# Loading an attention's values as fp32 rows and casting them on the engines, in a fused attention and MoE kernel with a hand-made order of work

## The chip, the cores and the metric

The kernel runs on one core of a Trainium2 chip. A core has five engines that each run their own list of instructions in order: TensorE (PE in the profile; its weight loads are shown as PEld), VectorE (DVE), ScalarE (ACT), GpSimd (POOL) and SyncE (SP). Sixteen DMA engines move data between HBM (the chip's DRAM) and SBUF (the core's memory, 128 partitions); PSUM is the small memory of eight banks into which TensorE writes. The metric is the device time of one execution in microseconds, as a median over runs.

## The reference

Two layers follow each other. First comes attention with a window, for 8 batches, 8 heads, 576 positions and 64 numbers a head:

```
scores = q @ k^T / sqrt(64) - slope[h] * |i - j|       where 0 <= i - j < 128, else -1e9
attn   = softmax(scores)                               per row
x      = attn @ v      -> transposed and reshaped to (8*576 = 4608 tokens, 512)
```

Then comes a feed-forward layer with a gate of its own:

```
h   = x @ w_in                                         (4608, 2048)
g   = h * sigmoid(beta * h)                            beta: one number for each of 2048 columns
out = g @ w_out                                        (4608, 512), float32
```

All inputs and the output are float32. The kernel multiplies in bf16 and accumulates in float32.

## The kernel before

The program is one long list of steps, the string PLAN (lines 18 to 126). A step such as `H:2:4:0` or `gv.s:1:0` names a helper, its engine where there is a choice (`.s` SyncE, `.p` GpSimd, `.v` VectorE, `.a` ScalarE) and its numbers. The loop at the end (line 716) goes through the list and issues each step on its engine. The place of a step in the list therefore sets the order on each engine, and nothing else reorders the work: an engine waits at a step until the data or the buffer that the step needs is there, and everything behind the step on that engine waits with it.

Attention works on one batch after the other. A batch has five blocks of positions, four of 128 and one of 64.

- **Queries and keys.** `gq` and `gk` (`get`, line 306) load a block of all heads as fp32 rows with a SyncE DMA into one of 14 buffers, tile `fst`. `cQ` and `cK` cast it to bf16 (`move`, line 205) on any of three engines. `D` (line 500) is a transposing DMA, also on SyncE, into `qkT`. In batches 0 and 1, which stand at the start, loads of head pairs (`k`, `q`, line 315) and transposes on TensorE (`Rk`, `Rq`) take their place.
- **Values.** In batches 0 to 2, `gv` loads fp32 rows into the same 14 buffers through SyncE, and `cv` casts them into `vs` (line 205). In batches 3 to 7 one step, `pv` (line 342), is a DMA issued by GpSimd that reads fp32 and writes bf16 straight into `vs`. There are two `vs` tiles; batch b writes the one that batch b-2 used, so both `cv` and `pv` wait until batch b-2 has been read.
- **Scores and weights.** `S` (line 522) multiplies, `E` (line 531) takes the exponential on ScalarE, `M` (lines 261 and 275) multiplies by the slopes' factors on VectorE, `V` (lines 574 and 577) multiplies with the values, `n` (lines 585 and 586) divides by the sums on VectorE, and `XD` (line 620) is a transposing DMA on SyncE that writes the tokens into `XT`, a ring of three groups of 512 tokens.

The feed-forward layer works on nine groups of 512 tokens. `H` (line 632) makes one of 16 column blocks of h with four matmuls of 512 columns; `a` (line 640, ScalarE) and `d` (line 645, VectorE) apply the gate; `O` (line 655) takes four matmuls of 512 columns for a quarter of a 128-token block of the output; `oc` (lines 677 and 679) copies it out of PSUM and `st` (line 684) stores it, from three engines. `OL` (line 666) is the last block in two halves. The weights come in eight GpSimd DMAs of 512 KB, `w1` (line 350) and `w2` (line 354), each needed by the first `H` or `O` that reads its part. `pad` (lines 285 to 287) is five memsets on GpSimd. `z` are matmuls on zeros that keep TensorE busy at the start.

So SyncE's queue carries most loads, all transposing DMAs of both kinds and some stores in one order, GpSimd's queue carries the weights, the casting loads of values and some stores, and TensorE's list mixes attention of batch b with the feed-forward layer of earlier tokens.

Of the kernel before, what the change touches and what calls it, by code (L numbers as in the profile page):

```python
# [18 lines left out]
k.s:0:2 const ck.a:0:2 k.s:0:0 k.s:0:1 q.s:0:0 beta:4 k.s:1:0 ck.p:0:0 cq.v:0:0 ones ck.a:0:1 z:2:2  # L19
q.s:0:1 ck.a:1:0 z:2:1 q.s:0:2 q.s:0:3 Rk:0:0:3 Rk:0:1:6 z:1:4 z:1:2 k.s:1:3 gv.s:0:1 k.s:0:3  # L20
cq.v:0:1 Rk:0:2:0 Rk:1:0:1 rk.a:0:0 Rq:0:1:2 cq.v:0:2 rq.a:0:1 Rq:0:2:3 q.s:1:0 q.s:1:1 ck.p:1:3
ck.p:0:3 rq.a:0:2 rk.v:0:1 rk.v:0:2 Rq:0:0:4 B:0:1:6:0 rk.v:1:0 rq.a:0:0 B:0:0:4:0 A:0:2:2:1 EB:0:1
MB:0:1 cv.p:0:1 fr:2 cq.v:1:0 cq.a:0:3 A:0:0:6:1 EB:0:0 EA:0:2 z:2:0 gv.s:0:0 EA:0:0 B:0:2:0:1
cv.p:0:0 Rk:0:3:5 MB:0:0 fr:6 A:0:1:2:1 Rq:0:3:4 Rk:1:3:6 rq.v:0:3 rk.a:0:3 B:0:3:4:1 EA:0:1 EB:0:2
cq.v:1:1 EB:0:3 w1:0 Rq:1:1:7 rk.v:1:3 VA:0:0:3 VA:0:1:0 Rq:1:0:2 VA:0:2:6 A:0:3:4:1 nA:0:0 order
rq.v:1:1 gv.s:0:3 rq.a:1:0 cv.p:0:3 gv.s:0:2 B:1:0:1:0 k.s:1:1 q.s:1:3 cv.p:0:2 w1:1 nA:0:1 nA:0:2
VB:0:2:7 EA:0:3 VB:0:3:5 nB:0:2 ck.a:1:1 VB:0:1:4 VB:0:0:3 Rk:1:1:0 A:1:0:6:1 EB:1:0 nB:0:0 cq.p:1:3
q.s:1:2 nB:0:1 cq.p:1:2 rk.a:1:1 k.s:1:2 EA:1:0 XP:0:2:3 XP:0:0:2 w1:2 VA:0:3:4 gq.s:0:4 xc.a:0:0
nB:0:3 nA:0:3 Rq:1:3:1 XP:0:1:0 xc.v:0:2 A:1:1:5:1 rq.a:1:3 XP:0:3:1 pad ck.p:1:2 EA:1:1 A:1:3:3:1
B:1:1:6:0 xc.a:0:1 xc.a:0:3 h:0:0:5:0:3 EB:1:1 fr:7 fr:5 fr:4 EA:1:3 MB:1:0 H:0:2:1 gv.s:1:2  # L30
h:0:0:5:3:4 h:0:1:7:0:3 H:0:3:2 Rq:1:2:3 h:0:1:7:3:4 Rk:1:2:6 MB:1:1 a:0:2 a:0:3 d:0:2 fr:3 gv.s:1:1
fr:1 rk.v:1:2 a:0:0 H:0:7:1 gv.s:0:4 gk.s:0:4 H:0:6:4 H:0:4:6 gv.s:1:0 d:0:3 d:0:0 fr:0 cQ.a:0:4
fl:0 a:0:7 rq.a:1:2 cv.p:1:2 A:1:2:2:1 a:0:6 d:0:7 a:0:4 H:0:10:5 gv.s:1:3 H:0:5:0 gk.s:1:4 a:0:1
H:0:8:1 d:0:6 EA:1:2 d:0:4 a:0:10 w1:3 a:0:5 ft cK.p:0:4 cv.p:0:4 d:0:1 cv.p:1:0 a:0:8 cv.a:1:1
B:1:2:2:1 d:0:10 EB:1:2 H:0:9:5 VA:1:2:6 gq.s:1:4 d:0:5 d:0:8 gv.s:2:4 gv.s:2:1 gk.s:2:0 VA:1:0:1
TT:0:7 H:0:11:4 cv.p:1:3 a:0:9 VA:1:1:0 a:0:11 nA:1:2 tt.v:0 nA:1:0 d:0:9 B:1:3:6:1 EB:1:3 VB:1:2:5
SCT:0:1 nA:1:1 w2:0 VB:1:0:0 gv.s:1:4 gq.s:2:0 VA:1:3:3 d:0:11 ECT:0 gk.s:2:1 cK.p:2:1 VB:1:1:4
gk.s:2:2 cv.p:1:4 H:0:14:7 nB:1:2 nB:1:1 h:0:15:1:0:2 cQ.a:1:4 gq.s:2:4 gk.s:2:4 a:0:14 cK.a:1:4
VB:1:3:4 w2:1 h:0:15:1:2:4 XP:1:1:2 nA:1:3 MCT:0 PV:0:0:6 nB:1:0 XP:1:2:3 PV:0:1:5 gq.s:2:2 cQ.p:2:2
xc.a:1:1 d:0:14 XP:1:0:0 xc.a:1:0 xc.a:1:2 TT:1:2 nV:0:1 nV:0:0 nB:1:3 a:0:15 H:0:12:7 H:0:13:0  # L40
tt.v:1 w2:2 X:0:4:3 a:0:13 XP:1:3:4 x.v:0:4 d:0:13 xc.a:1:3 SCT:1:5 H:1:7:2 ECT:1 a:1:7 H:1:14:0
d:0:15 a:0:12 fl:2 d:1:7 H:1:9:6 H:1:12:1 a:1:12 d:0:12 gq.s:2:1 gq.s:2:3 d:1:12 H:1:3:4 H:1:5:5
H:1:4:1 a:1:3 a:1:9 H:1:1:3 H:1:10:2 a:1:5 d:1:3 H:1:0:7 a:1:4 a:1:14 d:1:4 w2:3 a:1:1 a:1:10
cK.v:2:2 O:0:0:0:4 d:1:5 d:1:14 d:1:1 cQ.v:2:0 cQ.p:2:1 cv.p:2:4 d:1:10 cK.v:2:0 D:2:0 d:1:9
H:1:15:0 H:1:2:1 gq.s:3:1 D:2:2 a:1:2 a:1:0 H:1:13:5 cv.v:2:1 cQ.a:2:4 O:0:2:0:2 H:1:6:3 O:0:2:1:2
H:1:8:6 O:0:0:1:4 O:0:0:2:4 d:1:0 a:1:6 a:1:13 cK.a:2:4 gk.s:2:3 D:2:1 d:1:2 d:1:13 MCT:1 d:1:6
gv.s:2:0 O:0:2:2:2 O:0:3:0:3 gq.s:3:0 H:1:11:7 a:1:8 a:1:15 a:1:11 d:1:8 cQ.v:2:3 cv.p:2:0 d:1:15
gk.s:4:0 cQ.p:3:1 cK.v:2:3 d:1:11 O:0:0:3:4 O:0:2:3:2 O:0:3:1:3 D:2:4 D:2:3 S:2:0:0:0 S:2:0:1:5
oc.v:0:2 O:1:0:0:2 O:1:0:1:2 gv.s:2:3 E:2:0:1 E:2:0:0 gk.s:3:4 st.s:0:2 O:0:3:2:3 S:2:0:2:6 oc.v:0:0
S:2:0:3:4 PV:1:1:0 gk.s:3:0 E:2:0:3 O:1:0:2:2 E:2:0:2 gq.s:3:2 nV:1:1 fl:4 gv.s:2:2 M:2:0:3 M:2:0:2  # L50
O:0:3:3:3 fl:3 oc.v:0:3 S:2:1:3:4 E:2:1:3 M:2:0:1 fl:1 S:2:1:2:0 S:2:1:0:6 E:2:1:0 O:1:0:3:2
oc.a:1:0 M:2:1:3 E:2:1:2 S:2:1:1:4 M:2:0:0 gq.s:3:4 cv.p:2:2 cQ.v:3:0 M:2:1:0 O:0:1:0:3 E:2:1:1
PV:1:0:6 O:0:1:1:3 gq.s:4:1 gk.s:3:2 gk.s:4:4 gq.s:3:3 V:2:0:0 nV:1:0 cQ.p:3:4 M:2:1:2 O:1:1:0:2
V:2:1:4 n:2:0 O:1:2:0:7 gk.s:3:1 O:1:2:1:7 n:2:1 cQ.p:3:2 M:2:1:1 O:1:1:1:2 X:1:4:6 XD:2:0 XD:2:1
cv.a:2:3 pv:3:1 V:2:2:0 n:2:2 XD:2:2 O:1:2:2:7 O:1:1:2:2 V:2:3:4 O:1:2:3:7 x.a:1:4 cK.v:3:4
O:0:1:2:3 cK.v:3:0 n:2:3 oc.a:1:2 O:0:1:3:3 O:1:1:3:2 cK.v:3:2 cK.v:3:1 gk.s:3:3 st.a:0:0 V:2:4:5
H:2:4:0 H:2:1:7 D:3:0 D:3:2 n:2:4 gq.s:4:2 H:2:10:4 a:2:1 a:2:4 oc.a:0:1 D:3:1 oc.v:1:1 gk.s:4:2
H:2:3:1 H:2:5:6 d:2:4 H:2:2:0 d:2:1 H:2:0:7 D:3:4 a:2:5 H:2:7:3 st.s:1:0 a:2:10 d:2:10 a:2:2 a:2:3
cQ.p:4:1 a:2:0 a:2:7 gq.s:4:0 cK.p:3:3 cQ.v:3:3 d:2:2 d:2:5 d:2:3 H:2:9:4 O:1:3:0:2 a:2:9 cQ.p:4:0
S:3:0:0:5 S:3:0:2:0 O:1:3:1:2 d:2:0 d:2:7 gk.s:5:4 D:3:3 st.a:0:1 O:1:3:2:2 E:3:0:0 E:3:0:2  # L60
S:3:0:1:6 d:2:9 S:3:0:3:3 H:2:6:5 gk.s:4:1 H:2:11:1 O:1:3:3:2 H:2:8:0 E:3:0:1 pv:3:2 E:3:0:3 a:2:6
S:3:1:1:6 a:2:11 a:2:8 XD:2:3 H:2:12:4 E:3:1:1 d:2:6 d:2:11 cK.p:4:2 pv:3:0 cQ.v:4:2 a:2:12 H:2:13:5
d:2:8 M:3:0:1 d:2:12 oc.v:1:3 cK.p:4:0 S:3:1:0:0 E:3:1:0 H:2:14:6 M:3:0:3 M:3:0:2 S:3:1:3:3 a:2:14
S:3:1:2:0 d:2:14 E:3:1:3 O:2:0:0:2 O:2:0:1:2 E:3:1:2 D:4:0 gq.s:4:3 H:2:15:7 M:3:1:3 st.p:0:3
cK.p:4:1 pv:3:4 M:3:0:0 cQ.p:4:3 pv:4:0 st.p:1:2 a:2:15 a:2:13 M:3:1:1 M:3:1:0 d:2:15 O:2:2:0:3
O:2:0:2:2 pv:3:3 V:3:0:0 O:2:1:0:6 n:3:0 cK.v:4:4 d:2:13 M:3:1:2 O:2:1:1:6 V:3:1:0 n:3:1 O:2:1:2:6
V:3:2:4 O:2:1:3:6 n:3:2 gk.s:4:3 D:4:1 D:4:2 gq.s:4:4 gk.s:5:3 cK.v:4:3 cQ.p:4:4 O:2:0:3:2 O:2:2:1:3
st.a:1:1 oc.a:2:1 S:4:0:1:6 pv:4:1 S:4:0:3:4 S:4:0:2:0 E:4:0:1 O:2:2:2:3 E:4:0:3 O:2:3:0:7 E:4:0:2
XD:2:4 XD:3:0 XD:3:2 XD:3:1 oc.v:2:0 D:4:4 D:4:3 O:2:2:3:3 V:3:3:4 V:3:4:0 n:3:3 O:2:3:1:7 oc.v:2:2
O:2:3:2:7 n:3:4 H:3:2:4 H:3:0:2 a:3:2 S:4:0:0:5 d:3:2 a:3:0 gq.s:5:2 gq.s:5:0 M:4:0:1 H:3:7:0  # L70
E:4:0:0 d:3:0 a:3:7 O:2:3:3:7 H:3:1:5 d:3:7 oc.a:2:3 a:3:1 S:4:1:2:2 S:4:1:0:0 M:4:0:2 st.s:2:0
cQ.p:5:2 S:4:1:1:6 gk.s:5:1 E:4:1:0 d:3:1 E:4:1:1 H:3:6:4 H:3:4:5 a:3:6 E:4:1:2 H:3:3:1 XD:3:4
M:4:0:3 M:4:0:0 V:4:0:6 H:3:9:0 a:3:4 d:3:6 n:4:0 V:4:1:3 gq.s:5:1 XD:3:3 H:3:5:2 gk.s:5:2 pv:4:2
st.s:1:3 gq.s:5:3 H:3:12:7 gq.s:7:4 gk.s:5:0 XD:4:0 cK.a:5:1 a:3:3 n:4:1 a:3:9 M:4:1:0 H:3:8:3
XD:4:1 d:3:4 a:3:8 S:4:1:3:5 H:3:15:4 cK.p:5:2 E:4:1:3 d:3:3 pv:4:3 pv:4:4 a:3:12 d:3:9 H:3:14:0
a:3:14 a:3:5 d:3:8 pv:5:1 M:4:1:2 d:3:14 d:3:5 H:3:10:3 H:3:11:1 H:3:13:5 a:3:10 a:3:13 gq.s:5:4
H:4:1:2 H:4:4:6 H:4:2:0 cQ.p:5:3 a:3:11 cK.a:5:0 cQ.a:5:1 M:4:1:3 d:3:12 d:3:13 O:3:1:0:5 H:4:0:7
cQ.v:5:0 d:3:11 a:4:1 cK.p:5:3 cQ.p:5:4 D:5:2 a:3:15 st.s:2:1 a:4:2 gq.s:6:2 a:4:0 d:3:10 D:5:0
# [671 lines left out]
```

## Time and profile before

| | us |
|---|---|
| median of 3 runs (lowest to highest) | 324.43 (323.64 to 325.98) |
| the profiled execution | 323.59 |
| its span | 321.8 |
| TensorE busy | 307.9 (96%) |
| VectorE, ScalarE, GpSimd busy | 198.1, 186.3, 62.9 |
| value loads by GpSimd, 25 instructions | 21.1 |
| casts by GpSimd, 33 into `bst` and 12 into `vs` | 21.0 and 7.9 |

The span runs from the first to the last instruction of the program; the execution has 1.8 us around it. A busy TensorE is not TensorE at its full rate: the profile counts a matmul as busy from its issue to its modelled end, and matmuls overlap. The time to landing of a DMA counts from its issue by the engine, so it holds the wait behind the transfers ahead of it in the queue as well.

### The profile page before, as it was taken

The page shows a single profiled execution, that of the slowest core. Times are in us where ns is not written, and L with a number is a line of the kernel's source. Part 1 is how long each engine was busy: PE and PEld are TensorE (multiplying, and loading weights), DVE is VectorE, ACT ScalarE, POOL GpSimd, SP SyncE. Part 2 cuts the span into 40 slices and gives each one's busy share as a digit, 9 for nine tenths or more (in the row PEclk, how much of TensorE's full clock was granted, in tenths as well). Part 3 has the DMA queues.
Part 4 walks back from the last instruction along what each step waited for, and adds up shares of the span by engine and source line. Part 5 has one row for each costly group of instructions (what it writes and reads, how often), then busy time and mean ns, then how long its engine had stood idle before and what let it go on. Part 6 is the DMA issues. An engine that isn't in the chain of part 4 may idle for free.

```text
span 321.8 us, 5879 instructions
## 1 busy us (share of the span) xinstructions
PE 307.9 (96%) x2218; PEld 152.2 (47%) x2257; DVE 198.1 (62%) x391; ACT 186.3 (58%) x278; POOL 62.9 (20%) x101
## 2 busy tenths in 40 slices
PE   8899999979989999899999999999999999999995
PEld 3464554434544445354455444544544544444543
DVE  4789886843856494588755645752876536865102
ACT  7999786615407854479565664746469324773010
POOL 2372404101301631242050143112000000000000
PEclk9999999998999999999999999999999999999999
DMA  7999999999999999999999899599651134000023
GB/s 243 281 250 199 194 202 187 180 210 223 201 167 233 189 201 172 202 226 179 210 152 230 149 178 138 71 174 182 84 103 35 51 70 152 1 33 2 33 83 147
DMA packets 152684, 50.01 MB, mean 155 GB/s; under 512 B 140288, under 2 KB 148752, under 8 KB 152656
## 3 DMA queue, kind: packets, MB, share of 16 engines
q1 hardware_dynamic: 122512, 37.24, 63.2%
q0 software_dynamic: 28384, 9.51, 27.4%
q10 hardware_dynamic: 1760, 2.89, 2.5%
q8 instruction: 17, 0.28, 0.4%
q14 instruction: 11, 0.09, 0.1%
HBM read 36.71 MB, written 9.44 MB: 143 GB/s over the span
## 4 chain that ended last, share of the span: by engine, by line
PE 74%; DMA 12%; SPq 6%; DVE 2%; POOL 2%; issue 2%; ACT 1%; POOLq 0%; ACTq 0%
PE PS L632 33%; PE PS L655 30%; DMA XT<-xn 6%; PE PS L522 4%; DMA fst<-in_q_dram 3%; DMA fst<-in_k_dram 2%; SPq L500 2%; PE PS L577 2%; SPq L315 2%; PE PS L574 2%; SPq L306 1%; DMA qkT<-bst 1%; PE PS L666 1%; DVE bst L205 1%; PE PS L453 1%
## 5 line engine op out<-in xcount | busy, mean ns | idle before, releaser
L632 PE MATMUL PS<-XT,W 128*128 128x512 bf16 x558 | 132.3, 379 | 3.5 <-DMA XT<-xn 2.3
L640 ACT ACTIVATE sig<-PS,beta_h 128x512 bf16<-128x512 f32 x144 | 94.4, 688 | 68.6 <-PE PS L632 61.9
L655 PE MATMUL PS<-W,gT 128*128 128x512 bf16 x540 | 131.7, 382 | 1.4 <-issue 0.5
L645 DVE SCALAR_TENSOR_TENSOR gT<-sig,PS 128x512 bf16<-128x512 bf16 x144 | 94.0, 683 | 57.1 <-ACT sig L640 56.7
L632 PEld LDWEIGHTS <-W 128*128 128x128 bf16 x576 | 54.2, 98 | 66.9 <-issue 4.2
L655 PEld LDWEIGHTS <-gT 128*128 128x128 bf16 x560 | 52.6, 98 | 61.5 <-issue 3.7
L531 ACT ACTIVATE pt<-PS 128x1024 bf16<-128x1024 f32 x48 | 47.0, 1023 | 22.5 <-PE PS L522 22.1
L205 POOL CAST bst<-fst 128x512 bf16<-128x512 f32 (+1 forms) x33 | 21.0, 644 | 102.4 <-DMA fst<-in_q_dram 36.1
L677 ACT ACTIVATE osb<-PS 128x512 f32<-128x512 f32 (+1 forms) x20 | 11.3, 576 | 33.6 <-PE PS L655 24.0
L342 POOL DMA_DIRECT2D vs<-in_v_dram x25 | 21.1, 847 | 26.4 <-PE PS L577 26.4
L684 POOL DMA_DIRECT2D out_dram<-osb x9 | 5.1, 576 | 88.5 <-DVE osb L679 84.0
L679 DVE TENSOR_SCALAR osb<-PS 128x512 f32<-128x512 f32 x17 | 11.4, 686 | 17.2 <-PE PS L655 17.2
L586 DVE TENSOR_TENSOR xn<-PS,zb 128x512 bf16<-128x512 f32 (+1 forms) x30 | 20.7, 690 | 1.0
L275 DVE TENSOR_TENSOR pt<-pt,fall 128x1024 bf16<-128x1024 bf16 x24 | 16.0, 684 | 4.8 <-ACT pt L531 4.8
L585 DVE RECIPROCAL zb<-PS 128x8 f32<-128x8 f32 (+1 forms) x30 | 6.1, 202 | 19.0 <-PE PS L577 18.4
L205 DVE CAST bst<-fst 128x512 bf16<-128x512 f32 (+1 forms) x28 | 12.6, 455 | 7.1 <-DMA fst<-in_q_dram 2.7
L577 PE MATMUL PS<-vs,pt 128*128 128x65 bf16 x240 | 16.9, 193 | 0.0
L261 DVE TENSOR_TENSOR pt<-pt,falls 128x1024 bf16<-128x1024 bf16 x24 | 16.3, 700 | 0.9 <-ACT pt L531 0.8
L522 PE MATMUL PS<-qkT 64*128 64x256 bf16 (+2 forms) x240 | 14.9, 250 | 2.0 <-DMA qkT<-bst 1.8
L577 PEld LDWEIGHTS <-pt 128*128 128x128 bf16 x240 | 14.6, 97 | 3.5 <-DVE pt L275 0.2
L431 ACT ACTIVATE pt<-PS 128x1024 bf16<-128x1024 f32 (+1 forms) x16 | 14.3, 931 | 0.8 <-PE PS L421 0.6
L522 PEld LDWEIGHTS <-qkT 64*128 64x128 bf16 x240 | 8.7, 94 | 12.6 <-issue 12.1
(73 smaller groups left out, 171.9 us busy)
## 6 DMA issues: line engine op xcount, KB each, us to landing
fst<-in_k_dram SPq DMA_DIRECT2D x32, 256.0 KB, 4.8
fst<-in_q_dram SPq DMA_DIRECT2D x32, 256.0 KB, 5.2
out_dram<-osb SPq DMA_DIRECT2D x16, 256.0 KB, 3.1
fst<-in_v_dram SPq DMA_DIRECT2D x12, 256.0 KB, 6.2
vs<-in_v_dram POOLq DMA_DIRECT2D x20, 128.0 KB, 6.3
out_dram<-osb ACTq DMA_DIRECT2D x10, 256.0 KB, 3.0
out_dram<-osb POOLq DMA_DIRECT2D x9, 256.0 KB, 4.0
W<-in_moe_w_in_dram POOLq DMA_DIRECT2D x4, 512.0 KB, 9.0
```

Of the source, the lines that this page charges most:

```text
L205: (nc.scalar.copy if eng is nc.scalar else eng.tensor_copy)(out=out, in_=in_)
L261: nc.vector.tensor_tensor(out=pt[:], in0=pt[:], in1=falls[:, 2 * p : 2 * p + 2], op=ALU.mult)
L275: nc.vector.tensor_tensor(out=x, in0=x, in1=bass.AP(tensor=t.tensor, offset=t.offset, ap=[list(t.ap[0]), [P, 4], [0, 2], [1, P]]), op=ALU. ...
L342: return nc.gpsimd.dma_start(out=VS[b % 2][0:rows, sb, :, 0:D], in_=v[b, :, P * sb : P * sb + rows, :].rearrange("h p d -> p h d"))
L522: nc.tensor.matmul(o, lhsT=qk[64 * e : 64 * e + 64, 1, p, P * kb : P * kb + P], rhs=qk[64 * e : 64 * e + 64, 0, p, P * kb : P * kb + nq], ...
L531: nc.scalar.activation(out=pt[:], in_=held.pop(("S", b, m, p)), func=ACTF.Exp, scale=qscale)
L577: nc.tensor.matmul(o, lhsT=weights(b, qb, h, 0), rhs=vs[:, qb, h, 0 : D + 1], start=qb == 0, stop=True, skip_group_check=True)
L586: nc.vector.tensor_tensor(out=xn[0:nq].rearrange("p (g h) d -> p g h d", g=2), in0=pv[0:nq, :, :, 0:D], in1=zs[0:nq].broadcast_to([nq, 2, ...
L632: nc.tensor.matmul(hps, lhsT=W1[:, c, bass.ts(j, P)], rhs=XT[:, c, c0 : c0 + TOKG], start=(c == 0), stop=(c == NDM - 1),)
L640: nc.scalar.activation(out=sig[:], in_=hps, func=ACTF.Tanh, scale=beta_h[:, j : j + 1])
L645: nc.vector.scalar_tensor_tensor(out=gts[g][:, j, :], in0=held.pop(("H", g, j))[:], scalar=1.0, in1=hs.pop((g, j)), op0=ALU.add, op1=ALU.mult)
L655: nc.tensor.matmul(ops_, lhsT=gT[:, j, i * P : i * P + P], rhs=W2[:, j, :], start=(j == 0), stop=(j == NFF - 1),)
```

## The change

Only the list is different; no helper is touched. Its counts change as follows.

| steps | before | after |
|---|---|---|
| `pv`, casting loads of values by GpSimd | 25 | 0 |
| `gv.s`, loads of values as fp32 rows by SyncE | 15 | 40 |
| `cv` on GpSimd, VectorE, ScalarE | 12, 1, 2 | 24, 10, 6 |
| `cQ` and `cK` on GpSimd, VectorE, ScalarE | 27, 23, 14 | 31, 16, 17 |
| `st` on SyncE, GpSimd, ScalarE | 16, 9, 10 | 10, 14, 11 |
| `oc` on VectorE, ScalarE | 17, 18 | 20, 15 |

The work of TensorE is the same set of steps in both lists. Since the whole list was made anew, the order of all engines differs from the first step on. The lines of the diff that the prediction speaks of (removed and added ones, each group in its own order):

```
-nB:0:3 nA:0:3 Rq:1:3:1 XP:0:1:0 xc.v:0:2 A:1:1:5:1 rq.a:1:3 XP:0:3:1 pad ck.p:1:2 EA:1:1 A:1:3:3:1
...
-cK.v:2:2 O:0:0:0:4 d:1:5 d:1:14 d:1:1 cQ.v:2:0 cQ.p:2:1 cv.p:2:4 d:1:10 cK.v:2:0 D:2:0 d:1:9
-H:1:15:0 H:1:2:1 gq.s:3:1 D:2:2 a:1:2 a:1:0 H:1:13:5 cv.v:2:1 cQ.a:2:4 O:0:2:0:2 H:1:6:3 O:0:2:1:2
-H:1:8:6 O:0:0:1:4 O:0:0:2:4 d:1:0 a:1:6 a:1:13 cK.a:2:4 gk.s:2:3 D:2:1 d:1:2 d:1:13 MCT:1 d:1:6
...
-V:2:1:4 n:2:0 O:1:2:0:7 gk.s:3:1 O:1:2:1:7 n:2:1 cQ.p:3:2 M:2:1:1 O:1:1:1:2 X:1:4:6 XD:2:0 XD:2:1
-cv.a:2:3 pv:3:1 V:2:2:0 n:2:2 XD:2:2 O:1:2:2:7 O:1:1:2:2 V:2:3:4 O:1:2:3:7 x.a:1:4 cK.v:3:4
...
+rq.v:0:2 ck.p:0:1 cq.p:0:1 pad A:0:2:1:1 B:0:2:4:1 EA:0:2 rk.a:0:0 Rq:0:0:3 Rk:0:1:6 Rq:0:1:7
...
+q.s:1:3 B:0:3:1:1 w1:0 EB:0:3 Rk:1:0:7 gq.s:0:4 A:0:3:3:1 z:2:5 Rq:1:0:6 gq.s:1:4 VB:0:1:2 fr:3
...
+gk.s:2:0 d:1:10 gv.s:1:4 gk.s:2:4 gk.s:3:1 a:1:6 a:1:12 cK.a:2:2 cK.a:2:0 a:1:4 cv.v:1:4 d:1:6
+cQ.v:2:4 H:1:7:4 w2:1 cK.p:2:1 d:1:12 w2:2 w2:3 O:0:0:0:7 D:2:2 H:1:13:3 H:1:8:6 a:1:7 d:1:4 H:1:0:0
+gk.s:2:3 H:1:1:2 D:2:1 a:1:13 a:1:1 H:1:5:1 O:0:0:1:7 a:1:8 cQ.p:2:0 d:1:13 fl:1 d:1:1 a:1:5
+cK.p:2:4 d:1:8 gq.s:2:3 H:1:2:5 H:1:9:2 O:0:2:0:6 O:0:0:2:7 O:0:2:1:6 a:1:0 D:2:0 d:1:7 d:1:5
...
+gv.s:3:1 D:3:2 D:3:1 a:2:3 gq.s:4:1 a:2:5 a:2:4 D:3:3 a:2:12 d:2:3 d:2:4 XD:2:3 st.p:0:1 d:2:5
...
+XD:3:1 cK.a:5:1 O:2:2:0:4 V:3:2:0 gv.s:4:0 O:2:3:1:7 O:2:2:1:4 cQ.p:4:4 d:2:14 n:3:2 O:2:0:2:2
+E:4:0:3 E:4:0:1 M:4:0:1 O:2:3:2:7 cv.p:4:0 oc.a:2:0 D:4:3 XD:3:2 XD:3:0 S:4:0:2:0 E:4:0:2 cv.a:4:1
...
+O:4:2:3:5 M:6:0:0 E:6:0:3 D:6:4 gv.s:6:3 XD:5:2 gq.s:7:3 a:5:0 V:5:4:1 H:5:4:7 H:5:9:3 n:5:4 a:5:4
+S:6:1:3:4 d:5:11 XD:6:0 XD:5:3 gk.s:7:2 D:7:0 S:6:1:1:2 gk.s:7:3 O:5:1:0:1 H:5:13:6 d:5:14 E:6:1:3
```

## The prediction

> **What bounds the kernel now.** I read the page first: busy shares, slices and DMA queues.
>
> ```profile
> PE 307.9 (96%) x2218; PEld 152.2 (47%) x2257; DVE 198.1 (62%) x391; ACT 186.3 (58%) x278; POOL 62.9 (20%) x101
> ...
> DMA  7999999999999999999999899599651134000023
> ...
> q1 hardware_dynamic: 122512, 37.24, 63.2%
> q0 software_dynamic: 28384, 9.51, 27.4%
> ```
>
> TensorE is the busiest engine by far, and until about 220 us the DMA engines are as busy as it; the others have room. q1 holds what SyncE issues, q0 what GpSimd issues. Whether TensorE really sets the end is told by its waits and by the chain of work between 58 and 96 us (start, length, what).
>
> ```profile
> PE PS L632 <- DMA XT<-xn: 2.3, 3, 0.9
> PE PS L522 <- DMA qkT<-bst: 1.8, 1, 1.8
> ```
>
> ```profile
> 66.37 0.58 SPq L306
> ...
> 67.07 4.03 DMA qkT<-bst
> 71.10 0.14 issue
> 71.24 0.61 PE PS L522 x8
> ...
> 89.85 4.97 DMA XT<-xn
> 94.82 0.14 issue
> 94.95 1.24 PE PS L632 x5
> ```
>
> TensorE hardly waits, and where it does it waits for a transposing DMA that stands behind other loads in SyncE's queue. The third view is the table by stage (TensorE's granted clock is the figure after the engines).
>
> ```profile
> 60.00:80.00 20.00, 17.89 (x107) 8.04 (x108) 9.25 (x19) 8.34 (x11) 1.17 (x2) 0.91 1.18 205
> 80.00:160.00 80.00, 77.39 (x563) 37.65 (x574) 55.95 (x104) 47.64 (x69) 21.31 (x30) 1.00 1.41 198
> 160.00:240.00 80.00, 78.78 (x578) 38.95 (x587) 48.04 (x88) 47.91 (x69) 17.40 (x24) 1.00 1.02 148
> ```
>
> In 60 to 80 the mean clock is 0.91: the trace's clock record has 0.5 for 3.4 us from 72.0, right after the wait of 1.8. A wait of 1.1 us near 131 has no such stretch behind it.
>
> To place these losses I add up TensorE's work ahead of a step in the list (four 512-column matmuls 0.86 us, as in the chain; a score step 0.27; a value step 0.24 to 0.49; all of it 303.5 us, the same in both lists) and subtract it from the step's real start. This **lag** is 3.6 us at the first H, 4.9 at the first O, 7.1 at batch 2's first score, 9.05 at its fifth, 10.2 at group 2's first H, 12.0 at group 3's, 13.4 at group 6's approach, 14.2 behind it, and 14.4 at group 8. After the last matmul come 3.5 us of copy and store. So 303.5 + 14.4 + 3.5 is the span (321.8 with rounding). Everything that the new list can win or lose is lag.
>
> **The change part by part.** *Front.* The new list puts the five memsets of `pad` (0.52 + 0.53 + 0.52 + 0.55 + 0.29 = 2.4 us) and four more casts ahead of the first weight load on GpSimd. Its 12th load (the twelfth one lands at 13.0 now) is cast after them, then come four casts of 0.61: the weight load goes out at about 16.6 instead of 15.7. It took 8.4 us to land (24.1, when the first H started at 24.2), so it lands at 25.0. The new list has 19.9 us of TensorE work ahead of that H, the old 20.4; the lag there is 25.0 - 19.9 = 5.1 instead of 3.7. The old one rises to 4.9 by itself soon after, through a value cast that came late (0.5). I charge **+0.5**; bounds 0 (other stalls hidden behind it) and +2 (each of the four weight loads lands 3.4 us behind the one before, so all come late).
>
> *Batch 2's scores.* The three transposes that they need went out at 58.6, 60.8 and 67.1. SyncE stood 6.4 us ahead of the first one, for a cast that VectorE made only at 57.1, behind eight gate steps. In the new list these casts stand on GpSimd behind the weight loads and on ScalarE behind six gate steps of group 1; six H blocks after 41.2 us of work plus lag end near 52, so the casts end near 54. From there bounds differ. Early: all goes out 4.6 us sooner, lands at 66.5, and TensorE, which comes at 61.5 + 5.4 = 66.9, does not wait. Late: the DMA engines are full until then, nearly the same transfers are ahead (45 SyncE transfers instead of 46, about 0.6 us less), and the last lands at 70.5: a wait of 3.6. I take the middle, a wait of 2.1, and with it the half clock as in the trace (1.9): lag 5.4 + 2.1 + 1.9 = 9.4, that is +0.35 against 9.05, **-0.15 beyond the front's charge**; ends -4.0 and +1.5.
>
> *Waits at groups 2, 3 and 6.* They are 1.0, 1.1 and 0.7 us now. TensorE work between the last value step that such a group needs and its first H goes from 6.1 to 7.3, from 8.7 to 9.9 and from 9.7 to 8.0 us. The first two gain as much as they lacked, but fp32 value rows now go through the same queue; I take **-1.6** of 2.1. For the third I take 0 (bounds -0.7, +1.7).
>
> *GpSimd loses* 25 casting loads (25 x 0.847 = 21.1 us) and gets 12 value casts (12 x 0.666 = 8.0), 4 of queries and keys and 5 stores. It is 20% busy: 0. Its waits of 26.4 us for batch b-2's values go with the loads; the wait is then at the cast, and a cast of batch 3 to 7 has its rows in `fst` by then. What is late next is the buffer: 14 `fst` tiles serve 25 more loads than before, and a load with no free buffer holds all of SyncE.
>
> The Trainium skill ("SBUF — State Buffer", section "SBUF: two separate sides") warns that a DMA issued by GpSimd starves while VectorE runs its fast copies, about 3.1 us instead of 0.62, which speaks for the change. The row here disagrees: 25 issues at 685 to 942 ns, and 6.3 us to landing against 6.2 for SyncE's value rows. By the rule 25 x 2.5 us would be freed on GpSimd; by the row nothing that TensorE waits for.
>
> *VectorE and ScalarE* get 9 and 4 more value casts (0.42 and 0.61 us), but 7 fewer and 3 more of queries and keys, and copies of outputs move by three. That is about +2 us each on 198 and 186. In the fullest stage above they are 70% and 60% busy, and TensorE waited there 0.3 us in all for anything but DMA: 0; without that cover each cast delays the gate step behind it by its own length, 13 casts by some 6 us in all.
>
> *SyncE* gets 25 issues at 0.55 us (13.8) and loses 6 stores (some 3): +10.5 us of issue. From 80 to 220 us it is the queue that both transposes stand in.
>
> *The DMA engines.* The trace's packet records give 1024 packets a value block either way: 128-byte ones of q0 take 38.4 ns on average, 256-byte ones of q1 24.8 (18 when nothing else runs). Over 16 engines a block costs 2.46 us as a casting load, 1.59 as rows; 20 full and 5 half blocks: 22.5 x 0.87 = 19.6 us less engine time, from 88 us on. From the other side: where q0 runs alone it moves a packet every 22.6 ns, so the true saving may be a quarter of that. But q1 alone gets 22.5 x 1.59 = 35.8 us more, and it is at 0.95 to 1.03 busy in each of the five stretches of 20 us from 60 to 160. Sum on the path: 0, since the lag's waits are counted above; ends in the rivals.
>
> The same skill ("DMA: Bandwidth & Descriptors", "SWDGE vs HWDGE vs iDMA") says that an engine takes turns between the queues of GpSimd and of SyncE. That speaks against the change: what took turns with a transpose now stands ahead of it. No row here separates the two; by the rule each transpose with one value block newly ahead is up to 1.6 us later.
>
> *Tail.* The last output block and its halves end both lists: 0.
>
> Sum: 323.59 + 0.5 - 0.15 - 1.6 + 0 = 322.3 for the profiled execution's kind. The median shown is 0.84 above it: 323.2. I take **323.5**, rounding towards the queue's side.
>
> **The rivals.** *Faster:* the early end holds at batch 2 (no wait, no half clock: -4.0) and the three waits go (-2.8), with +0.5 in front: 324.4 - 6.3 = 318. For it: the old stall came from one late cast, and less DMA time. Against: the DMA slices are full up to 70 us in any order.
>
> *Slower, the single queue:* place, SyncE's queue from 80 to 160 us; the values of batches 3 to 5, 13.5 blocks' worth, are 21 us more in a queue that has some 4 us free. If its packets stay at 24.8 ns, the last transposes before group 5 come 17 us late, less about 2 to 4 us that TensorE has in hand at each score and H step and 4 that the lag covers already: 9 to 10 us, 334. If they fall to 18 ns it costs nothing; it decides from about 22 ns on. For it: landing takes 4 to 5 us for 1.2 us issues, so the queue is never empty. Against: the sum of packets is the same in both.
>
> *Slower, the list:* the change does not act through values; the weights come 2 us late, batch 2's scores wait 3.6 and every gain at groups 2 and 3 is eaten: 324.4 + 2 + 1.5 + 0.7 = 328.6.
>
> **How the numbers follow.** About no change (323.5, 321.2 to 327.6) has 0.48; faster 0.20; slower 0.32, of it 0.20 for the queue and 0.12 for the list. A difference under 1% is about what a measurement of this kernel cannot tell from none. The range leaves out the last tenth on each side: from the faster case's 318 with VectorE's and start's noise, 317.5, to nearly the queue's 334, 333.
>
> **What would show it.** Right: the lag at batch 2's fifth score step near 9.4, a half clock near 70 us once, waits for `XT` under 1 us in all, q1's 256-byte packets under 22 ns. Wrong: waits of TensorE for `qkT` or `XT` between 100 and 170 us, a second stretch of half clock, SyncE held at a value load for want of a buffer, or gate steps of VectorE that wait behind value casts.

## The result, and the profile after

The changed kernel takes 326.87 us (median of 9 runs, 324.97 to 328.06). The kernel before, run between them, takes 324.97 us (9 runs). The ratio is 1.0071, 95% interval 1.0045 to 1.0097. So the change makes the kernel 0.7% slower; I had forecast 0.3% faster. The profiled execution took 325.81 us with a span of 324.0 us, 2.2 us more than before. Lines move by 4 because the list is longer: L632 is now L636, L522 is L526, L205 is L209.

The page of the changed kernel, the same parts as shown of before: busy time by engine, the DMA slices, and the two queues.

```profile
PE 307.1 (95%) x2217; PEld 151.7 (47%) x2257; DVE 201.0 (62%) x394; ACT 187.4 (58%) x280; POOL 59.8 (18%) x101
...
DMA  6999999999999999999999999969352041001024
...
q1 hardware_dynamic: 145088, 41.57, 71.1%
q0 software_dynamic: 5344, 7.87, 11.4%
```

The load moved as planned: 23,000 packets left GpSimd's queue (q0) and 22,600 more stand in SyncE's (q1). TensorE's waits (line, what for: us in total, times, longest):

```profile
PE PS L373 <- ACT bst L209: 2.3, 1, 2.3
PE PS L581 <- ACT pt L535: 1.9, 1, 1.9
PE PS L425 <- DVE qkT L209: 1.4, 2, 0.7
...
PE PS L526 <- DMA qkT<-bst: 0.9, 2, 0.7
```

The waits for `XT` (2.3 us before) are gone, and that for `qkT` is half of what it was. Two new ones stand on top, both for ScalarE: from 5.5 us (a cast) and from 119 us (exponentials). The table by stage (after the engines: TensorE's granted clock, DMA share, GB/s):

```profile
0.00:20.00 20.00, 13.95 (x109) 6.33 (x112) 10.69 (x33) 13.56 (x24) 11.97 (x27) 0.91 0.96 265
...
60.00:80.00 20.00, 19.89 (x112) 8.94 (x112) 13.19 (x25) 11.57 (x18) 3.00 (x5) 1.00 1.27 206
80.00:160.00 80.00, 76.50 (x572) 37.92 (x581) 53.57 (x100) 49.11 (x72) 12.78 (x19) 1.00 1.16 205
160.00:240.00 80.00, 78.98 (x565) 38.50 (x574) 51.25 (x92) 47.48 (x71) 18.71 (x29) 1.00 0.96 180
```

The stretch from 60 to 80 us, the bad one before (busy 17.89, clock 0.91), is now full. The stretch of half clock moved to the start (it lasts 3.4 us, from 7.7 us on), and 80 to 160 us lost 0.9 us of TensorE's busy time.

The prediction's lag (real start of a step minus the TensorE work ahead of it in the list) shows where the 2.2 us arise:

| step | lag before | after | change in the stretch that ends here | predicted |
|---|---|---|---|---|
| first H | 3.6 | 8.5 | | |
| batch 2's first score | 7.13 | 10.32 | +3.2 | +0.5 |
| batch 2's fifth score | 9.05 | 10.54 | -1.7 | -0.15 |
| group 2's first H | 10.18 | 10.75 | -0.9 | -1.6 (this row and the next) |
| group 3's first H | 11.97 | 14.48 | +1.9 | (see above) |
| group 8's first H | 14.40 | 16.88 | 0.0 | 0 |

The sum is +2.5; what follows group 8's first H is 0.3 us shorter. Two stretches lose: the beginning and the one from group 2 to group 3.

**The beginning.** The new list's fourth load is a key pair that TensorE needs at once; TensorE waits 2.3 us for its cast on ScalarE, runs at half clock for 3.4 us, and waits 2.3 us more in three pieces for copies by VectorE and exponentials by ScalarE. The first weights landed at 26.2 us, but TensorE came only at 28.4.

**Group 2 to group 3.** The chain of work of the changed kernel between 111 and 122 us (start, length, what):

```profile
111.08 3.14 SPq L624
114.22 0.05 issue
114.27 0.58 SPq L310
114.85 0.05 issue
114.90 0.57 SPq L310
115.47 0.04 issue
115.51 3.93 DMA fst<-in_k_dram
119.44 0.67 ACT sig L644
120.11 0.92 ACT pt L535
121.04 0.04 issue
121.08 0.41 PE PS L581 x8
```

and ScalarE's timeline there (start, length; in brackets the idle time before and what ended it):

```profile
114.09 1.28 ACT L644 ACTIVATE sig<-PS,beta_h 128x512 bf16<-128x512 f32 x2
118.91 0.62 ACT L209 CAST vs<-fst 128x512 bf16<-128x512 f32 x1 [3.54 <-DMA fst<-in_v_dram]
119.43 0.68 ACT L644 ACTIVATE sig<-PS,beta_h 128x512 bf16<-128x512 f32 x1
120.01 1.93 ACT L535 ACTIVATE pt<-PS 128x1024 bf16<-128x1024 f32 x2
```

A transposing DMA holds SyncE for 3.14 us. Only then go out the rows of value blocks 2 and 0 of batch 3 (114.27 and 114.90); block 0 lands at 118.89. ScalarE has its cast next in order and stands still for 3.54 us. Behind it are a gate step and two exponentials, and for these TensorE waits 1.9 us. (The chain names a key load issued just behind; the timeline names the value rows.)

### The profile page after: what moved, and what is told of

Its sections match the earlier page's. It is cut to its first block, busy times and chain, and to the rows that moved or that the text cites. A ratio compares the mean times of both kernels' runs of the same rounds, so it can differ in the third digit from the quotient of the medians.

```text
span 324.0 us, 5913 instructions
## 1 busy us (share of the span) xinstructions
PE 307.1 (95%) x2217; PEld 151.7 (47%) x2257; DVE 201.0 (62%) x394; ACT 187.4 (58%) x280; POOL 59.8 (18%) x101
## 4 chain that ended last, share of the span: by engine, by line
PE 71%; DMA 8%; SPq 7%; issue 2%; ACT 2%; POOL 1%; DVE 0%; ACTq 0%; POOLq 0%; DVEq 0%
PE PS L659 31%; PE PS L636 30%; DMA fst<-in_k_dram 5%; SPq L310 3%; PE PS L526 3%; PE PS L581 2%; SPq L504 2%; DMA fst<-in_q_dram 2%; PE PS L578 2%; SPq L624 1%; DMA qkT<-bst 1%; PE PS L670 1%; ACT sig L644 1%; POOL vs L209 1%; ACT pt L535 1%
## 5 line engine op out<-in xcount | busy, mean ns | idle before, releaser
L636 PE MATMUL PS<-XT,W 128*128 128x512 bf16 x558 | 131.3, 379 | 1.0
L659 PE MATMUL PS<-W,gT 128*128 128x512 bf16 x541 | 128.6, 379 | 1.5 <-issue 0.6
L636 PEld LDWEIGHTS <-W 128*128 128x128 bf16 x576 | 54.1, 98 | 63.7 <-issue 1.7
L535 ACT ACTIVATE pt<-PS 128x1024 bf16<-128x1024 f32 x48 | 47.0, 1022 | 21.1 <-PE PS L526 21.0
L209 POOL CAST bst<-fst 128x512 bf16<-128x512 f32 (+1 forms) x41 | 27.6, 688 | 98.7 <-DMA fst<-in_q_dram 49.2
L683 DVE TENSOR_SCALAR osb<-PS 128x512 f32<-128x512 f32 x20 | 13.8, 688 | 27.3 <-PE PS L659 27.3
L681 ACT ACTIVATE osb<-PS 128x512 f32<-128x512 f32 (+1 forms) x17 | 9.7, 573 | 36.2 <-PE PS L659 26.3
L209 POOL CAST vs<-fst 128x512 bf16<-128x512 f32 (+1 forms) x24 | 16.3, 687 | 56.8 <-DMA fst<-in_v_dram 48.9
L688 POOL DMA_DIRECT2D out_dram<-osb x14 | 7.6, 544 | 101.8 <-DVE osb L683 66.2
L265 DVE TENSOR_TENSOR pt<-pt,falls 128x1024 bf16<-128x1024 bf16 x24 | 17.9, 753 | 6.9 <-ACT pt L535 6.8
L209 ACT CAST bst<-fst 128x512 bf16<-128x512 f32 (+1 forms) x21 | 12.6, 616 | 11.5 <-DMA fst<-in_k_dram 11.2
L581 PE MATMUL PS<-vs,pt 128*128 128x65 bf16 x240 | 17.2, 193 | 1.9 <-ACT pt L535 1.9
L435 ACT ACTIVATE pt<-PS 128x768 bf16<-128x768 f32 (+1 forms) x16 | 14.4, 919 | 5.0 <-PE PS L425 4.5
L526 PE MATMUL PS<-qkT 64*128 64x256 bf16 (+2 forms) x240 | 15.2, 250 | 1.0 <-DMA qkT<-bst 0.9
L578 PE MATMUL PS<-vs,pt 128*128 128x65 bf16 x192 | 14.8, 193 | 0.1
```

The costliest lines, as they stand in the source:

```text
L209: (nc.scalar.copy if eng is nc.scalar else eng.tensor_copy)(out=out, in_=in_)
L265: nc.vector.tensor_tensor(out=pt[:], in0=pt[:], in1=falls[:, 2 * p : 2 * p + 2], op=ALU.mult)
L526: nc.tensor.matmul(o, lhsT=qk[64 * e : 64 * e + 64, 1, p, P * kb : P * kb + P], rhs=qk[64 * e : 64 * e + 64, 0, p, P * kb : P * kb + nq], ...
L535: nc.scalar.activation(out=pt[:], in_=held.pop(("S", b, m, p)), func=ACTF.Exp, scale=qscale)
L578: nc.tensor.matmul(o, lhsT=weights(b, qb - 1, h, 1), rhs=vs[:, qb - 1, h, 0 : D + 1], start=True, stop=False, skip_group_check=True)
L581: nc.tensor.matmul(o, lhsT=weights(b, qb, h, 0), rhs=vs[:, qb, h, 0 : D + 1], start=qb == 0, stop=True, skip_group_check=True)
```

## The experiments

The experiments test three theories: **A**, the value rows cost the time, in its narrow form the one cast that waits on ScalarE ahead of exponentials; **B**, the new list's beginning costs it; **C**, SyncE's queue has no room for 25 more loads, whatever their order. Each ratio is to the kernel before, run on the same chip in the same set; the brackets hold a 95% interval. The changed kernel itself was not run again in these sets, so it is compared through its own ratio, 1.0071. Every profile is one execution, and some of them lie well off their kernel's median; where that matters it is said. Diffs show steps of the list; an unchanged neighbour marks the place.

### Taking the values back

`e1_pv_back`, for all 25 blocks of batches 3 to 7:

```
-gv.s:3:1 ... cv.p:3:1
+             pv:3:1
```

> The new list, with the values of batches 3 to 7 as casting loads by GpSimd again: each of the 25 casts becomes the casting load at its own place, the 25 loads through SyncE are gone. Theory A (the value rows cost the time: ScalarE waits 3.5 us for batch 3's rows near 118 us, and TensorE waits 1.9 us behind it): the lag no longer rises by 2 us there, 2 us less than the new kernel, ratio to the old one about 1.000. Theory B (the list's new front costs it, 4.8 us at the first H, of which some stays to the end): as the new kernel, ratio 1.006 to 1.008. Theory C (the one queue of SyncE is too full): more than 2 us less, waits for transposes go as well.

325.03 us, ratio 1.0007 (0.9975 to 1.0039). The loss is gone as far as this interval tells. Nothing else of the new list was undone, so without the rows and their casts it is about as fast as the old one.

`e10_only3_back` does this for batch 3 alone, `e11_4to7_back` for the others alone.

> The changed kernel with the values of batch 3 alone again as casting loads of GpSimd at the places of their casts; those of batches 4 to 7 stay fp32 rows on SyncE's queue. Theory A (one place: the rows of batch 3 that land at 118.9 us): the whole loss goes, 325.0 us, ratio to the kernel before 1.001, lag from group 2's first H to group 3's up by some 2.8 instead of 3.7. Theory C (25 more loads in a full queue, wherever they stand): only the share of batch 3 goes, 326.3, ratio 1.005.

> The other half of the same cut: the values of batches 4 to 7 again as casting loads, those of batch 3 as fp32 rows. Theory A: the wait of 1.9 us near 119 stays and with it the loss, 326.8, ratio 1.007. Theory C: most of the loads are out of the queue, 325.4, ratio 1.003.

0.9989 (0.9960 to 1.0018) and 1.0038 (1.0005 to 1.0072). Taking back the five blocks of batch 3 removes the whole loss. Taking back the 20 others removes about half of it by the middle value, and the interval allows anything from nearly none to nearly all: 1.0038 is closer to theory C's 1.003 than to theory A's 1.007. Together the two shares, 0.8% and 0.3%, are more than the loss. So the medians put the loss at batch 3 first, as theory A says, but not there alone. The profile of the former doesn't show the gain at that place. Its wait at 119 is gone, but from 110 us on TensorE waits for a transposing DMA,

```profile
PE PS L521 <- DMA qkT<-bst: 2.1, 1, 2.1
```

half clock follows for 3.4 us, and the lag rises by 4.6 us from group 2 to group 3, more than the changed kernel's 3.7.

### One cast, one order, one queue

`e5_one_cast_gpsimd` moves the waiting cast off ScalarE:

```
-cv.a:3:0
+cv.p:3:0
```

> The new list with one engine changed: the cast of batch 3's first value block on GpSimd instead of ScalarE. Theory A in its narrow form (a cast that waits for its rows ahead of exponentials and gate steps): TensorE's wait of 1.9 us near 119 us goes, 1.5 to 2 us less than the new kernel, ratio 1.001 to 1.002. Theories B and C: no change, ratio 1.006 to 1.008.

1.0083 (1.0046 to 1.0119), nothing gained. TensorE's waits:

```profile
PE PS L522 <- DMA qkT<-bst: 2.7, 2, 1.6
...
PE PS L577 <- POOL vs L205: 1.2, 1, 1.2
```

TensorE now waits for GpSimd's cast of the same rows, and more for transposes. `e16_order_only` leaves the cast on ScalarE but lets it and its reader stand later:

```
-V:3:0:4 E:3:1:0
+E:3:1:0 cv.a:3:0
...
+V:3:0:4 n:3:0 O:2:3:0:7
```

> The changed kernel with two steps moved and nothing else: ScalarE's cast of value block 0 of batch 3 stands behind the last exponential of that batch instead of ahead of two of them, and TensorE's value step that reads it stands behind two more output blocks. The rows land as late as before. Theory A in its narrow form (the wait comes from work queued behind the waiting cast): the loss near 119 goes, 325.1, ratio 1.001. Theory C (the queue has no room): the time stays with other late transfers, 326.5, ratio 1.005 or above.

1.0061 (1.0032 to 1.0090). The wait at 119 did go: from group 2 to 3 the lag rises by 2.3 instead of 3.7. But it rises by 2.4 between group 5 and batch 6's scores, where that of the changed kernel rises by 0.3. (This execution, 328.67 us, was the slowest of the 12, so the second rise may not be typical.) TensorE's waits in the whole run:

```profile
PE PS L522 <- DVE gT L645: 2.2, 3, 1.4
PE PS L522 <- DMA qkT<-bst: 1.5, 2, 1.0
```

So the narrow form of A falls, by the ratios of both runs: taking the work from behind the waiting cast doesn't bring the time back.

`e6_rows_of_3_early` lets the two row loads and two loads of batch 4's queries change places:

```
-gq.s:4:3   -gq.s:4:0   -gv.s:3:2 gv.s:3:0
+gv.s:3:2   +gv.s:3:0   +gq.s:4:3 gq.s:4:0
```

> The changed kernel with two pairs of SyncE's loads exchanged: the rows of value blocks 2 and 0 of batch 3 take the places of the query rows of blocks 3 and 0 of batch 4, some 12 and 8 us of TensorE work earlier, and those query rows take theirs. The number of transfers stays. Theory A (the loss is these rows landing at 118.9 us, behind which a gate step and two exponentials stood): the wait of 1.9 us near 119 goes and nothing takes its place, 325.0 us, ratio to the kernel before 1.001. Theory C (SyncE's one queue has no room for 25 more loads, whatever their order): another transfer is late instead, 326.5 or more, ratio 1.005 or above, with waits for qkT or XT in place of the one that goes.

Much slower, 329.75 us, 1.0166 (1.0117 to 1.0216). The value step has no wait now (the lag at batch 4's first score is 12.2 instead of 14.4), but the query rows come late, SyncE stands from 115.3 to 119.2 us for their casts, a key load behind lands at 131.45, ScalarE waits 7.7 us for that one, and behind its cast stand exponentials again, with half clock after it:

```profile
PE PS L522 <- ACT pt L531: 3.2, 1, 3.2
```

So the same chain came back with another load (in the fastest of the six executions, 327.85 us): this exchange gave one load an early place at the cost of another, as theory C expects. Other orders were not tried.

`e15_rows3_by_scalare` gives batch 3's five row loads to ScalarE's DMA queue, `e9_rows_by_gpsimd` gives all 25 to GpSimd's:

```
-gv.s:3:0           -gv.s:3:0 ... gv.s:7:4
+gv.a:3:0           +gv.p:3:0 ... gv.p:7:4
```

> The changed kernel with the five loads of batch 3's value rows issued by ScalarE on its own DMA queue at their places in the list; the same transfers, casts and everything else. If the rows are late because they stand in SyncE's one queue behind transposes (Theory A with the queue as its cause), they go out some 4 us sooner and land by 116, the wait near 119 goes: 325.0, ratio to the kernel before 1.001. If they are late because the DMA engines are full, or if the issues delay ScalarE's exponentials, 326.5 or more, ratio 1.005 or above.

> The changed kernel with the 25 loads of fp32 value rows of batches 3 to 7 issued by GpSimd at their places in the list, not by SyncE; rows, casts and all else stay. Theory C (the one queue of SyncE): transposes and rows are early again, 325.0, ratio 1.001 or below, and no wait near 119. Theory A (where the rows stand in the order, not whose queue it is): GpSimd comes to the loads of batch 3 as late as SyncE or later, a wait stays, 326.5 or more, ratio 1.005 or above.

The first: 325.47 us, 1.0025 (0.9999 to 1.0051). Block 0's rows went out at 109.6 instead of 114.9 and landed at 117.4:

```profile
117.43 0.62 ACT L205 CAST vs<-fst 128x512 bf16<-128x512 f32 x1 [2.12 <-DMA fst<-in_v_dram]
```

TensorE's wait at the value step is 0.4 us, and the lag rises by 1.7 us from group 2 to group 3 instead of 3.7. Same bytes, same casts, another queue: by the middle value that is two thirds of the loss, and this trace (the fastest of the 12 executions) shows the gain at its place. But the rows took 7.8 us to land instead of 4.0: going out 5.3 us earlier brought them 1.5 us earlier, so their place in SyncE's queue is not all that held them. The second missed every expectation: 337.5 us, 1.0327 (1.0256 to 1.0398). It is no clean test of theory C, because the rows travel in other packets there (the last section).

### The values alone, in the old list

`e2_rows_old_list` has nothing of the new list but this, for 25 blocks, the load about 10 us of TensorE work ahead of its cast:

```
-               pv:3:1
+gv.s:3:1 ...   cv.p:3:1
```

> The old list with the values alone changed: each casting load of batches 3 to 7 becomes a cast by GpSimd at the same place, and SyncE gets a load of fp32 rows about 10 us of TensorE work ahead of it. Nothing else of the new list is there. Theory A and C (the values' rows cost the time): slower, 326.5 to 329, ratio 1.005 to 1.013, with waits for qkT, XT or vs between 100 and 170 us. Theory B (the rest of the new list costs it): no change, 324.7, ratio 1.000.

332.72 us, 1.0249 (1.0205 to 1.0293). TensorE's waits:

```profile
PE PS L632 <- DMA XT<-xn: 4.7, 2, 2.9
PE PS L522 <- DMA qkT<-bst: 2.6, 2, 1.7
PE PS L522 <- DVE gT L645: 2.4, 1, 2.4
```

The lag grows from 12.1 at group 2 to 21.1 at batch 6 (before: 10.2 to 13.2). At these places, which I chose crudely, the 25 row loads and their casts on GpSimd cost 8 us; the new list, with the same loads at other places, loses only 2.

### The beginning

`e3_old_front_new_rest` and `e4_new_front_old_rest` join one list's beginning (up to group 1's first H) to the other's rest:

```
 e3: old list up to group 1's first H + the new list's remaining steps
 e4: new list up to group 1's first H + the old list's remaining steps, its pv
```

> The old list up to the first H of group 1, and the new list for everything behind it. Theory B (front): 1.5 to 2.5 us less than the new kernel, ratio 1.000. Theory A (values): TensorE comes to batch 2's first score 5 us sooner, waits there for the same transposes until about 71 us and gets the half clock as the old kernel did, so nothing is won, ratio 1.006 to 1.009, and the wait near 118 us is there as before.

> The new list up to the first H of group 1, and the old list, casting loads and all, behind it. Theory B (front): 1.5 us or more above the old kernel, ratio 1.005 to 1.008. Theory A (values): the lag is 10 us instead of 5 at the first O, but the wait and the half clock at batch 2's scores (4 us) and the wait at group 2 (1 us) go, so it ends within 0.5 us of the old kernel, ratio 1.000 to 1.002.

1.0151 (1.0104 to 1.0198) and 1.0116 (1.0074 to 1.0157), both slower than either parent. In the first the seam made its own stall: TensorE waits 4.3 us for a gate step and runs at half clock for 6.8 us from 56.9. They say little about the beginning.

`e7_front_swap` exchanges two loads of the changed kernel; `e8_pv_back_front` does so in `e1_pv_back` and moves two weight loads:

```
-q.s:0:1 k.s:0:2            -cv.p:0:1 ... cv.p:0:3 ... w1:0 ... w1:1
+k.s:0:2 q.s:0:1            +w1:0 w1:1 cv.p:0:1 ... cv.p:0:3
```

> The changed kernel with two of SyncE's first loads exchanged (the key pairs of batch 0's third head pair third, the query pairs of the second head pair fourth), so that the cast which TensorE waits 2.3 us for at 5.5 us comes some 1.4 us earlier. Both theories on the front expect a wait of about 1 us there, no half clock behind it, and a lag at the first H near 6 instead of 8.5. Theory B (the new list's beginning costs the time): all of it stays, 324.3 us, ratio 0.998. Theory A and C: batch 2's first score step starts at 71.8 us because its transposes land at 71.75, so TensorE only waits longer there: 326.5 to 327, ratio 1.005 to 1.008.

> The new list with the values of batches 3 to 7 again as GpSimd's casting loads (as in e1_pv_back), with the two first loads exchanged as in e7_front_swap, and the first two weight loads ahead of GpSimd's casts of values 1 and 3 of batch 0 (1.2 us earlier). Theory B: the front's lag was what kept e1_pv_back from winning: 322.0, ratio 0.991. Theory A and C: the front is hidden behind batch 2's transposes: 325.0 as e1_pv_back, ratio 1.000.

1.0079 (1.0043 to 1.0116) and 0.9985 (0.9952 to 1.0018). Neither differs from its parent by more than the intervals. The wait of 2.3 us for ScalarE's cast shrank to 1.1 and 0.2, but in the first TensorE waits 1.4 us for one by GpSimd instead, and half clock came all the same, 10.2 us from 11.3 and 6.8 us from 13.8; the lag at the first H was 11.3 and 10.2, no better.

So `e13_warm` and `e14_warm_front` fill the waits of the first 15 us with idle matmuls on zeros, on top of `e10_only3_back`; the second also takes over the edits of `e8_pv_back_front` (and 5, 4, 3, 2, 4 instead of the counts below):

```
+z:10:1 Rk:0:2:5   +z:3:1 A:0:2:1:1   +z:2:0 Rk:0:1:6   +z:2:0 B:0:0:6:0   +z:4:2 A:0:0:6:1
```

The counts shown add 21 idle matmuls. The second kernel has 18 (the expectation misstates this as 22, and the last one as 17).

> e10_only3_back with 21 idle matmuls (4.5 us of TensorE work) put into the places in the first 15 us where TensorE waits for casts and copies. If the half clock that follows these waits costs the new list time at its end (Theory B), it goes, the lag at the first H falls below 7.8 counted without the added work, and the time is 323.0, ratio 0.995. If the added work itself delays the copies' readers as much as it saves, or batch 2's transposes take the gain, 324.5 or more, ratio 0.999 or above.

> As e13_warm (22 idle matmuls), and in front of it the exchange of two first loads and the two earlier weight loads of e8_pv_back_front. Theory B: the best of all, 322.5, ratio 0.994. Otherwise 324.2, ratio 0.998.

1.0012 (0.9985 to 1.0040): no gain from the idle matmuls alone. With the earlier loads **323.21 us, 0.9958 (0.9941 to 0.9974): the fastest of all, and below both kernels.** The first 24 us (the granted clock is the figure after the engines) of the kernel before, the changed kernel and this one:

```profile
0.00:24.00 24.00, 20.93 (x224) 11.51 (x227) 16.46 (x55) 20.59 (x36) 11.07 (x25) 1.00 1.04 258
```

```profile
0.00:24.00 24.00, 17.58 (x176) 8.91 (x179) 13.99 (x45) 16.98 (x29) 14.12 (x30) 0.93 1.02 249
```

```profile
0.00:24.00 24.00, 20.77 (x195) 10.69 (x196) 14.22 (x45) 16.78 (x29) 14.46 (x30) 1.00 1.03 254
```

The 18 idle matmuls, some 3.9 us, are part of the 20.77 us of busy time. The clock alone doesn't explain the gain: the profile of `e10_only3_back`, to which these edits were added, has a clock of 1.00 there as well.

Last, the same beginning with all rows on SyncE's queue (`e17_rows_warm_front`) and with all values as casting loads (`e18_pv_back_warm_front`), one set:

```
 after          + the edits of e14_warm_front's beginning
 e1_pv_back     + the edits of e14_warm_front's beginning
```

> The changed kernel, all value rows on SyncE's queue, with the beginning of e14_warm_front (two loads exchanged, two weight loads earlier, 22 idle matmuls). If the beginning and the values act independently, the gain of e14_warm_front over e10_only3_back (0.3%) comes off the changed kernel's ratio: 1.004, 326.0 us, and the wait behind batch 3's rows near 119 stays. If TensorE, coming earlier, only waits longer for these rows and transposes (Theory C), it stays at 1.007, 326.8.

> The same beginning with the values of batches 3 to 7 all back as casting loads (e8_pv_back_front and 17 of TensorE's idle matmuls more). Against e14_warm_front it differs only in the values of batches 4 to 7. If their rows cost nothing (Theory A), 323.2, ratio 0.996; if each row load costs a share (Theory C), 322.4, ratio 0.993.

0.9975 (0.9945 to 1.0004) and 0.9973 (0.9945 to 1.0001). I had expected 1.004 for the first. In this set the kernel before took 326.22 us, more than in the others (324.4 to 325.0), so the ratios compare and the times don't. With the beginning mended the 25 row loads cost nothing that these runs can tell. In the first one's profile SyncE is 1.8 us earlier at batch 3's rows, and ScalarE's cast comes at

```profile
117.51 0.62 ACT L205 CAST vs<-fst 128x512 bf16<-128x512 f32 x1 [2.30 <-DMA fst<-in_v_dram]
```

instead of 118.91; TensorE's wait there is 0.8 us.

### Batch 2's casts

In the changed kernel SyncE stood 9.9 us for a cast of batch 2's keys that ScalarE made at 60.0 us behind gate steps:

```profile
SPq L504 <- ACT bst L209: 9.9, 1, 9.9
```

`e8_pv_back_front` has the same stand, and `e12_batch2_casts` moves this cast and one more of it to GpSimd:

```
-cK.a:2:2 cK.a:2:0
+cK.p:2:2 ... cK.p:2:0
```

> e8_pv_back_front with two casts of batch 2's keys (blocks 2 and 0) moved from ScalarE, where they ran at 60.0 and 60.5 us behind gate steps while SyncE stood from 50.7 to 60.7 us for them, to GpSimd, which is idle from 54 to 69 us. If that stand delays batch 2's first score step, its transposes go out by 55 us and land some 3 to 5 us earlier; with a lag near 8 in front the step starts near 69.5 instead of 71.7: 322.5, ratio 0.993. If the DMA engines are the limit there (the four second-layer weight loads land until 66.5 us), nothing changes: 324.2, ratio 0.999.

327.70 us, 1.0092 (1.0057 to 1.0126): slower than its parent by 1%. The first transpose goes out at 50.7 instead of 60.6 us, and batch 2's first score step starts at 76.7 instead of 71.7. The DMA issues from 48 to 78 us (KB each, median us to landing), first of the parent, then of this kernel:

```profile
W<-in_moe_w_out_dram POOLq DMA_DIRECT2D x4, 512.0 KB, 11.0
...
qkT<-bst SPq DMA_TRANSPOSE x5, 5.2
```

```profile
W<-in_moe_w_out_dram POOLq DMA_DIRECT2D x4, 512.0 KB, 16.0
...
qkT<-bst SPq DMA_TRANSPOSE x4, 10.5
```

In this execution, the slowest of seven, weight loads and transposes both take longer where they run beside each other, and the transposes land at 69.6, 74.0 and 76.6 us instead of 67.1, 69.1 and 71.3.

## Why the prediction was wrong

Its sum was -1.25 us of lag; +2.5 came. Two of its terms failed: the front (+0.5, it came to +3.2) and the waits at groups 2 and 3 (-1.6, they came to +1.0). Step by step:

- **Front, +0.5: wrong, +3.2.** The step took the first weights' landing for what TensorE waits for (25.0 forecast, 26.2 found; the lag at the first H 5.1 and 8.5). It never asked whether TensorE would be there: the order of the first loads and casts, with the half clock behind the wait, held it 2.2 us beyond the weights. Mending it takes the loss away (1.0071 to 0.9975).
- **Batch 2's scores, -0.15: right in direction by luck, -1.7.** I had forecast a wait of 2.1 us and a half clock behind it. The casts came at 60.5, not near 54, and the last transpose landed at 71.75, later than my late end. There was still no wait, since TensorE itself came only at 71.81. So part of the front's loss is given back here: the last of the three lands near 71 in both kernels, and front and batch 2 together are +1.5. With the casts early (`e12_batch2_casts`) they landed later still, so in that beginning the late cast wasn't what held them.
- **Waits at groups 2, 3, -1.6: wrong, +1.0.** The waits for `XT` went as forecast (2.3 us to none of note; up to group 2 the lag gains 0.9). Then the rows took more than the whole gain at one place, +1.9 by group 3. Of this step's two halves the second, "fp32 value rows now go through the same queue", had been priced at half a microsecond.
- **GpSimd 0: right.** The fear for the 14 buffers didn't come true: SyncE's largest waits at a load (L310) are 3.3 and 3.2 us in all, against 10.5 (five waits, L306) before.
- **VectorE and ScalarE 0: wrong in kind.** I priced a cast without cover at its own length, 0.4 to 0.6 us. ScalarE stood 3.54 us at the one that waited, and so did the gate step and the exponentials behind it: what a cast passes on is the lateness of its rows.
- **SyncE's issue and DMA engines 0: wrong at one place.** The rival of the single queue named this stretch, 80 to 160 us: at batch 3 the rows stand behind a transpose that holds SyncE for 3.1 us, and about 2 us were lost there, not that rival's 9 to 10. Its 334 us are near the 332.72 of `e2_rows_old_list`, but that is the old list, for which it wasn't meant. From group 3 on there is no further loss.
- **Group 6 and the tail, 0: right in the sum.** The wait for `XT` at group 6 went as well, but from group 3 to group 8 the lag grows by 2.4 us in both.

The row by which I weighed it, q1's 256-byte packets, came out at 24.1 ns on average (24.8 before), not under 22. The 18 ns that I gave for packets when nothing else runs is the median packet in both traces; before, those of q1 with no packet of another queue beside them average 23.0 ns, so a fall to 18 was never near. The Trainium skill ("DMA: Bandwidth & Descriptors", "SWDGE vs HWDGE vs iDMA") says that an engine goes round between the queues of GpSimd and of SyncE. My estimate from that, a transpose up to 1.6 us later for a value block newly ahead of it, pointed the right way: taken once it would have turned my -1.6 into about 0, nearer to the +1.0 that was found. No run here shows the turn-taking by itself.

What is shown: with the new list's own beginning the value rows cost the time, those of batch 3 first (`e1_pv_back` and `e10_only3_back` by their ratios, `e15_rows3_by_scalare` also at its place in the trace); with the mended beginning they cost nothing that can be told (`e17_rows_warm_front` against `e18_pv_back_warm_front`). So the loss needs both. Not shown is that the beginning by itself is worse than the old list's: where the rows are back as casting loads, mending it moves the ratio from 1.0007 to 0.9973, with overlapping intervals, and the same edits were not tried on the old list. What stays open: why the two don't add up. Removing the first gives 0.8%, the second 1.0%, both 1.1%. The profiles suggest that a late TensorE in front also makes the transposes ahead of the rows late, so that either remedy brings the rows just in time, but the 1.4 us between the two casts are read from one execution each. It isn't settled either which of the three edits of `e14_warm_front`'s beginning carries the gain; alone or in pairs they gave none that can be told.

## What to carry to other kernels

When a load moves from another engine's queue into a full one, look at what stands ahead of it at its tightest place, and not only at its issue time and its bytes; and a cast behind it passes the lateness of the load, not its own length, to everything queued on its engine. When a list is remade, walk its first 20 us step by step: who is waited for, and does the clock fall? Two remedies for one loss need not add up.

## What the runs showed of the hardware

- **Half clock comes in pieces of 3.4 us, and short waits can bring it.** In the profiles the stretches, those at the very end aside, last 3.4, 6.8, 10.2 or 13.7 us. Of 13 kernels with the new beginning (one profile each), 10 have one in the first 24 us, of the 4 with idle matmuls in its waits none, and of the 3 with the old beginning none. In `e8_pv_back_front` it starts at 13.8 us, after waits of 1.2, 0.7 and 0.6 us; behind the changed kernel's wait of 1.9 us at 119 us there is none. The Trainium skill ("TensorE: Matmul & The Clock Gate", "Part 1: The HAM clock gate") gives a free-running window of 3.4 us, which agrees, and half rate after at least one idle window, which these short waits don't fill; there the runs differ from it.
- **With rows in GpSimd's queue, transposes were slower.** In `e9_rows_by_gpsimd` the 25 loads are 1,840 packets of 3.2 KB on average (5.90 MB); through SyncE the same bytes are 23,440 packets of 252 bytes on average. The DMA issues from 100 to 136 us, changed kernel, then this one:

```profile
qkT<-bst SPq DMA_TRANSPOSE x9, 4.1
...
XT<-xn SPq DMA_TRANSPOSE x5, 3.9
```

```profile
qkT<-bst SPq DMA_TRANSPOSE x7, 6.4
XT<-xn SPq DMA_TRANSPOSE x4, 6.8
```

  This is one of the longer executions of that kernel (343.5 us), and over the whole of it the medians are 4.8 and 3.9 us against 4.2 and 3.9. The Trainium skill ("DMA: Bandwidth & Descriptors", "Queues, rings and completion order") says that an engine goes round its queues packet by packet; longer turns of the other queue would fit these rows and those beside the weight loads in `e12_batch2_casts` (1 KB packets), but this is not shown: no run here changes the packet size alone.
